# Six first-layer steps made ahead and held, first k by two queues, masks shared with GpSimd, the activation-table request moved, new order

## The chip, the cores and the metric

The kernel runs on one core of one Trainium2 chip. The metric is the device time of one execution in microseconds (us). TensorE is PE in the profile, VectorE DVE, ScalarE ACT, GpSimd POOL, and SyncE's queue of transfers SP.

## The reference

Attention with a window and a few global keys, then a gated two-layer network on the result:

```python
scores = scale * np.matmul(q, k.transpose(0, 1, 3, 2))       # 4 batches, 8 heads, 768 rows, 64 wide
bias = -slopes[:, None, None] * dist[None, :, :]             # dist: |row - column|, or n_local for global keys
scores = np.where(keep, scores + bias, -1000000000.0)
a = np.exp(scores - np.max(scores, axis=-1, keepdims=True))
a = a / (np.sum(a, axis=-1, keepdims=True) + 1e-09)
x = np.matmul(a, v)                                          # as 3072 tokens of 512
h = x @ w_in                                                 # 512 -> 2048
sp = np.where(h > 20.0, h, np.log1p(np.exp(np.minimum(h, 20.0))))
out = (h * np.tanh(sp)) @ w_out                              # 2048 -> 512
```

## The kernel before, in words

The 3072 tokens are cut into 12 chunks of 256 rows (three to a batch). For a chunk there are 8 attention pieces of two heads and 128 rows each: `scores` (PE), `largest` (DVE: adds the mask, takes the row's extreme), `exps` (ACT: `Exp` with the row sum), a turn of the matrix, and `weigh` (PE, with v). The first three chunks do this in f32 and turn on PE; later ones split every factor into a high and a low f16 half (`high_a` on ACT or DVE, `low_a` on POOL or DVE) and turn by DMA.

The network takes a chunk in 8 steps, so there are 96 steps, numbered m. A step makes 256 hidden columns:

- `moe_in` (i): 24 matmuls into the PSUM tile `ph`, of which there are two.
- `exp_h` (j), `square_e` (u), `ln_u` (n), `inverse_u` (r): four ACT instructions of 128x512, with the functions Exp, Square, Ln and Exp, in this order for every step (lines 548, 552, 556, 560).
- `times_h` (G) and `times_r` (H) on DVE, the latter waiting for `inverse_u`.
- `high_g` (z) and `low_g` (Z): two f16 halves; then `moe_out` (o): 24 matmuls into the output's sums.

The weights come as 32 raw pieces of 64-bit words and are converted on the chip, by `exponent_w`, `sign_w`, `bits_w`, `join_w`, `high_w` and `low_w` on ACT, DVE and POOL (A, S, B, C, D, E); that stands beside the attention of the first chunks (the last piece's halves are written at 144 us).

Which instruction stands where on each engine is written out by hand: a string `PROGRAM` of some two thousand tokens is read from left to right. A token is a letter (the function) with a number (the step or piece), and a stroke after it picks the second engine (DVE in place of ACT for copies, DVE in place of POOL for low halves). The order of the tokens is the order on each engine. `J`, `e` and some other letters below are tokens of this kind.

The built program loads a table set for ACT's functions with an instruction of its own, ACT_TABLE_LOAD. Line 141 asks for one set, named for both Ln and Exp, ahead of everything. Where no such request covers a function, the toolchain puts a load in by itself. In the kernel before, the built program has one row ACT_TABLE_LOAD on ACT, that of line 141.

Of the kernel before, what the change touches and what calls it, by code (L numbers as in the profile page):

```python
# [11 lines left out]
F16 = mybir.dt.float16  # L12
# [8 lines left out]
P = 128  # L21
# [93 lines left out]
def windowed(st, tc, loc):  # L115
# [16 lines left out]
    WB = 4  # L132

# [7 lines left out]
    nc.scalar.preload_act_table_set("natural_log_exp_and_others")  # L141
# [21 lines left out]
    def load_qk(G):  # L163
        if G >= 2 * NC:
            return
        ci, g = divmod(G, 2)
        b, c = divmod(ci, NCHB)
        o = OWN if c == 0 else 0
        pairs = slice(g * GH // 2, (g + 1) * GH // 2)
        qr = raws.tile([P, GH // 2, CH], F32, name="qr", bufs=4)  # L170
        kr = raws.tile([P, GH // 2, KW], F32, name="kr", bufs=4)
        nc.sync.dma_start(qr, L.qT[b].rearrange("(a j) d s -> (j d) a s", j=2)[:, pairs, c * CH:(c + 1) * CH])
        for j in range(2):
            half = slice(j * D, (j + 1) * D)
            nc.sync.dma_start(kr[half, :, o:], L.kd[ci, half].rearrange("p (a j) w -> p a j w", j=2)[:, pairs, j, o:])
        raw[G] = (qr, kr)
# [73 lines left out]
    jj = mt.tile([P, P], F32, name="u")  # L250
# [5 lines left out]
    d0 = mt.tile([P, P], F32, name="r")  # L256
    k0 = mt.tile([P, P], F32, name="r")
# [5 lines left out]

    def masks_own():
        nc.vector.tensor_scalar(off, rel, 0.0, None, op0=ALU.is_lt)
        nc.vector.scalar_tensor_tensor(off, rel, L.nlf, off, op0=ALU.is_ge, op1=ALU.max)
# [4 lines left out]
        nc.vector.scalar_tensor_tensor(d0, k0, FAR, d0, op0=ALU.mult, op1=ALU.max)  # L271

    def masks_far():

# [6 lines left out]

    def mask_own(h, other=False):
        copy(mb0[:, h, :], d0, -L.slopes[h] * UNIT, other)

    def mask_far(h, other=False):
        copy(mb[:, h, :], rel, -L.slopes[h] * UNIT, other)
# [258 lines left out]

    def exp_h(m):
# [76 lines left out]
    def checks(i):  # L623
# [32 lines left out]
        "i": moe_in, "j": exp_h, "u": square_e, "n": ln_u, "r": inverse_u, "G": times_h, "H": times_r,  # L656
# [217 lines left out]
```

## Time and profile before

| what | value |
| --- | --- |
| median of 3 runs | 626.84 us (624.49 to 627.2) |
| the profiled execution's own time | 625.97 us |
| its span, first to last instruction | 624.2 us |
| PE, DVE, ACT, POOL busy | 97%, 72%, 72%, 25% of the span |
| ACT_TABLE_LOAD | 1, of 1283 ns, at 0.82 us |
| ACT's four functions of a step | 96 times each |

The profile counts an engine as busy while an instruction of its runs; waits and the issue of transfers are not counted. A wait is put down to what ended it. Matmuls are pipelined and their ends modelled, so a busy PE is not a PE at its peak. Line numbers are those of the kernel before.

### The profile page before, as it was taken

To read this page: it belongs to the slowest core of one execution; us is meant where nothing else is said; L and a number is where in the kernel's file an instruction comes from. 1 tells how busy PE (TensorE), PEld (TensorE's weight loads), DVE (VectorE), ACT (ScalarE), POOL (GpSimd) and SP (SyncE) were. 2 spreads that over 40 slices of the span, in tenths; PEclk is the share of its full clock that TensorE was granted. 3 is DMA by queue.
4 is the path that set the end of the run, shared out by engine and by line. 5 is a ranking of instruction groups with operands and counts; after the bars stand their busy time and mean duration, and the time that the engine had idled before them with its cause. 6 is when DMAs were issued, how large, how long until landed. Compare 5 with 4: busy or idle time off the path is not lost.

```text
span 624.2 us, 13611 instructions
## 1 busy us (share of the span) xinstructions
PE 605.9 (97%) x5066; PEld 418.3 (67%) x5066; DVE 448.8 (72%) x1192; ACT 451.3 (72%) x1109; POOL 154.2 (25%) x130
## 2 busy tenths in 40 slices
PE   5999999989999999999999999999999999999996
PEld 3887766646766675667666677666667667667672
DVE  6999998995798677884659796657785685542443
ACT  4999988696777777877776774669757877545652
POOL 0021343341301322423141122112123344111020
PEclk9999999999999999999999999999999999999999
DMA  8997763422595574748088668045342256300001
GB/s 216 323 264 248 220 192 102 125 64 54 100 209 130 119 157 85 117 82 196 1 191 153 112 136 174 35 96 128 60 67 84 55 95 132 81 1 1 34 1 37
DMA packets 123014, 73.02 MB, mean 117 GB/s; under 512 B 91712, under 2 KB 112192, under 8 KB 122944
## 3 DMA queue, kind: packets, MB, share of 16 engines
q1 hardware_dynamic: 122944, 72.11, 49.6%
q8 instruction: 41, 0.67, 0.5%
q14 instruction: 29, 0.24, 0.1%
HBM read 39.85 MB, written 6.29 MB: 74 GB/s over the span
## 4 chain that ended last, share of the span: by engine, by line
PE 79%; DVE 11%; DMA 5%; ACT 3%; issue 2%; DVEq 0%; ACTq 0%
PE po L586 34%; PE ph L541 34%; PE sc L399 5%; PE pav L478 4%; DMA wts<-w_out 3%; DVE ws L349 2%; DMA qr<-qT 2%; DVE ws L345 1%; DVE wts L154 1%; DVE gf L564 1%; PE pav L586 1%; DVE A L413 1%; PE po L452 1%; DVE gf L568 1%; DVE ws L339 1%
## 5 line engine op out<-in xcount | busy, mean ns | idle before, releaser
L541 PE MATMUL ph<-xT,wts 128*128 128x256 f16 x2304 | 264.5, 273 | 0.9 <-DVE gf L564 0.8
L541 PEld LDWEIGHTS <-wts 128*128 128x128 f16 x2304 | 222.9, 98 | 36.6 <-issue 2.8
L586 PE MATMUL po<-wts,gt 128*128 128x512 f16 x1056 | 241.2, 381 | 3.2 <-DVE wts L154 1.3
L586 PEld LDWEIGHTS <-gt 128*128 128x128 f16 x1152 | 110.4, 98 | 128.8 <-issue 8.2
L154 POOL TENSOR_TENSOR gt<-gf,gt 128x512 f16<-128x512 f32 x59 | 71.6, 1215 | 226.4 <-ACT gt L150 99.1
L548 ACT ACTIVATE e<-ph 128x512 f32<-128x512 f32 x96 | 56.7, 590 | 87.0 <-PE ph L541 86.0
L568 DVE CUSTOM_DVE_ANT_0 gf<-gf,r 128x512 f32<-128x512 f32 x96 | 77.8, 811 | 56.6 <-ACT r L560 53.5
L422 ACT ACTIVATE A<-A,nm 128x256 f32<-128x256 f32 (+1 forms) x192 | 91.4, 478 | 21.8 <-DVE nm L413 19.4
L564 DVE SCALAR_TENSOR_TENSOR gf<-e,ph 128x512 f32<-128x512 f32 x96 | 65.3, 681 | 35.3 <-ACT e L548 35.2
L413 DVE CUSTOM_DVE_ANT_0 A<-sc,mb 128x256 f32<-128x256 f32 (+1 forms) x192 | 68.0, 396 | 24.5 <-PE sc L399 22.7
L154 POOL TENSOR_TENSOR hl<-A,hl 128x512 f16<-128x512 f32 (+1 forms) x37 | 44.1, 1197 | 147.7 <-DVE hl L148 93.6
L560 ACT ACTIVATE r<-r 128x512 f32<-128x512 f32 x96 | 60.0, 625 | 2.1
L552 ACT ACTIVATE u<-e 128x512 f32<-128x512 f32 x96 | 59.9, 626 | 2.0
L556 ACT ACTIVATE r<-u 128x512 f32<-128x512 f32 x96 | 59.7, 624 | 1.9
L154 POOL TENSOR_TENSOR wts<-ws,wts 128x512 f16<-128x512 f32 x17 | 21.3, 1260 | 75.8 <-ACT wts L150 56.1
L422 ACT ACTIVATION_READ_ACCUMULATOR A<-A,nm 128x1 f32 x192 | 36.1, 188 | 0.0
L150 ACT ACTIVATE gt<-gf 128x512 f16<-128x512 f32 x41 | 25.3, 620 | 13.5 <-DVE gmax L568 12.3
L478 PEld LDWEIGHTS <-AT 128*128 128x128 f16 x792 | 28.7, 98 | 6.9 <-issue 2.1
L154 DVE TENSOR_TENSOR gt<-gf,gt 128x512 f16<-128x512 f32 x37 | 27.3, 739 | 3.8 <-ACT gt L150 3.6
L489 DVE CUSTOM_DVE_ANT_1 x<-pav,ri 128x512 f32<-128x512 f32 x24 | 16.6, 691 | 17.4 <-PE pav L478 15.0
L148 DVE TENSOR_SCALAR hl<-A 128x512 f16<-128x512 f32 (+1 forms) x37 | 15.6, 424 | 17.8 <-ACT A L422 13.2
L399 PE MATMUL sc<-wc,ws 64*128 64x256 f16 (+1 forms) x432 | 28.1, 262 | 0.1
(114 smaller groups left out, 606.2 us busy)
## 6 DMA issues: line engine op xcount, KB each, us to landing
kr<-kd SPq DMA_DIRECT2D x32, 208.0 KB, 4.8
qr<-qT SPq DMA_DIRECT2D x24, 256.0 KB, 4.0
wts<-w_in SPq DMA_DIRECT2D x12, 512.0 KB, 8.4
wts<-w_out SPq DMA_DIRECT2D x12, 512.0 KB, 8.8
out<-ob SPq DMA_DIRECT2D x11, 512.0 KB, 3.2
vr<-v SPq DMA_DIRECT2D x9, 512.0 KB, 4.2
vc<-vo SPq DMA_DIRECT2D x15, 192.0 KB, 3.3
kr<-kd SPq DMA_DIRECT2D x16, 144.0 KB, 4.1
```

Of the source, the lines that this page charges most:

```text
L154: (nc.vector if other else nc.gpsimd).tensor_tensor(out, in_, high, op=ALU.subtract)
L399: nc.tensor.matmul(sc[j][:, a2, 0:w], x[half, a2, rows_], y[half, a2, col0:col0 + w], start=(n == 0), stop=(n == len(terms) - 1))
L413: nc.vector.tensor_tensor_reduce(out=A[:, j, 0:w], in0=sc[j][:, 0:w], in1=m, scale=-1.0 / (UNIT if ci < CF32 else UNIT * SQ), scalar=3.0e3 ...
L422: nc.scalar.activation(A[:, j], A[:, j], AF.Exp, bias=nm[:, h:h + 1], scale=-1.0, accum_out=rs[:, h:h + 1])
L541: nc.tensor.matmul(ph[:, j, :].rearrange("p (b t) -> p b t", b=2), wv4[:, 2 * fb, x, c * P:(c + 1) * P], xT[:, :, y * NCC + c, :], start=( ...
L548: nc.scalar.activation(mish[m]["e"], mish[m]["h"], AF.Exp, scale=-1.0 / (SV * SW), accum_out=esum[:, m:m + 1])
L552: nc.scalar.activation(u, mish[m]["e"], AF.Square, bias=0.5)
L556: nc.scalar.activation(mish[m]["r"], mish[m]["u"], AF.Ln, bias=0.25 / RS, scale=1.0 / RS)
L560: nc.scalar.activation(r, r, AF.Exp, scale=-1.0)
L564: nc.vector.scalar_tensor_tensor(gf, mish[m]["e"], 0.5, mish[m]["h"], op0=ALU.add, op1=ALU.mult)
L568: nc.vector.tensor_tensor_reduce(out=gf, in0=gf, in1=mish[m]["r"], scale=SG / (SV * SW * RS), scalar=0.0, op0=ALU.mult, op1=ALU.max, accum ...
L586: nc.tensor.matmul(pos[ci][t], gt[:, x, j, t * P:(t + 1) * P], wv4[:, 2 * fb + 1, y, :], start=(fb == 0 and n == 0), stop=(fb == NFB - 1 a ...
```

## The change

- The request for the table set is no longer made ahead of everything: it has become a token, `e`, and stands once, as `e0`, behind the last token of the program.
- Layer 1 of steps 16 to 21 (the third chunk's first six) is made early, among the steps of the first two chunks. Its result is copied out of PSUM by the new function `hold_h` (J) into SBUF, two of the copies into the output's buffer `ob`, four into tiles `hs`; `exp_h` and `times_h` of those steps then read it there. Two of the copies to `ob` and two to `hs` are ACT's, two to `hs` DVE's.
- The second half of the first k comes by ACT's queue instead of SP's.
- The masks' outside test is made in two parts, the own block's first, and with the stroke the masks of heads 4 to 7 are made by POOL in place of DVE.
- `ln_u` and `inverse_u` work in place in `u` (three buffers) instead of a tile `r` (two); q and k have three raw buffers instead of four.
- The order of `PROGRAM` is new up to about step 83, with other choices of engine; from there on the tokens are the same.

```diff
+    HELD = range(2 * NFP, 2 * NFP + 6)
...
-    nc.scalar.preload_act_table_set("natural_log_exp_and_others")
...
-        qr = raws.tile([P, GH // 2, CH], F32, name="qr", bufs=4)
-        kr = raws.tile([P, GH // 2, KW], F32, name="kr", bufs=4)
+        qr = raws.tile([P, GH // 2, CH], F32, name="qr", bufs=3)
+        kr = raws.tile([P, GH // 2, KW], F32, name="kr", bufs=3)
...
-            nc.sync.dma_start(kr[half, :, o:], L.kd[ci, half].rearrange("p (a j) w -> p a j w", j=2)[:, pairs, j, o:])
+            (nc.scalar if G == 0 and j else nc.sync).dma_start(kr[half, :, o:], L.kd[ci, half].rearrange("p (a j) w -> p a j w", j=2)[:, pairs, j, o:])
...
+    def outside(cols):
+        nc.vector.tensor_scalar(off[:, cols], rel[:, cols], 0.0, None, op0=ALU.is_lt)
+        nc.vector.scalar_tensor_tensor(off[:, cols], rel[:, cols], L.nlf, off[:, cols], op0=ALU.is_ge, op1=ALU.max)
...
+    def masked(out, in_, h, other):
+        if other and h >= H // 2:
+            nc.gpsimd.tensor_scalar(out, in_, -L.slopes[h] * UNIT, None, op0=ALU.mult)
+        else:
+            copy(out, in_, -L.slopes[h] * UNIT, other)
...
+    def hold_h(m, other=False):
+        k = m - HELD[0]
+        if k < 2:
+            if k == 0:
+                obs["h"] = mt.tile([P, 2, DM], F32, name="ob", bufs=1)
+            hs = obs["h"][:, k].rearrange("p (j t) -> p j t", j=2)
+        else:
+            hs = mt.tile([P, 2, CH], F32, name="hs", bufs=len(HELD) - 2)
+        copy(hs, mish[m]["h"], 1.0, other)
+        mish[m]["h"] = hs
...
-        u = mish[m]["u"] = mt.tile([P, 2, CH], F32, name="u")
+        u = mish[m]["u"] = mt.tile([P, 2, CH], F32, name="u", bufs=3)
...
-        mish[m]["r"] = mt.tile([P, 2, CH], F32, name="r")
+        mish[m]["r"] = mish[m]["u"]
...
+        "e": lambda i: nc.scalar.preload_act_table_set("natural_log_exp_and_others"),
...
-        u95 G95 n95 z94 r95 o93 Z94 H95 z95 o94 k1 Z95' o95 k2 Q11
+        u95 G95 n95 z94 r95 o93 Z94 H95 z95 o94 k1 Z95' o95 k2 Q11 e0
```

Where ACT's instructions stand in the built programs. First the start of ACT in the kernel before: L141 is the request for the set, L150 a helper's copy (`mb` are masks), L422 `exps`.

```order
L141 ACT_TABLE_LOAD
L150 ACTIVATE mb_99<-r 128x128 x2
L150 ACTIVATE mb<-e 128x256 x2
L150 ACTIVATE mb_99<-r 128x128
L422 ACTIVATE A,rs_163<-A,nm_164 128x128 x4
```

The same place in the changed kernel, where `exps` is line 430:

```order
L175 DMA kr<-kd 64x2x288
L150 ACT_TABLE_LOAD
L150 ACTIVATE mb_98<-u 128x128 x3
L150 ACTIVATE mb<-e 128x256
L150 ACTIVATE mb_98<-u 128x128
L430 ACTIVATE A,rs_147<-A,nm_148 128x128 x2
```

The load has moved behind ACT's own transfer, and it now belongs to line 150, a copy: it is one that the toolchain put there.

The second place is the last two steps on ACT, where the tokens of the two programs are the same. Before, L548, L552, L556 and L560 are Exp, Square, Ln and Exp of a step (the numbers behind the names tell the buffers apart), and `gt` is a copy of `high_g`:

```order
L548 ACTIVATE e_8361,esum_105<-ph_8308 128x512
L552 ACTIVATE u_8363<-e_8361 128x512
L556 ACTIVATE r_8367<-u_8363 128x512
L560 ACTIVATE r_8367<-r_8367 128x512
L548 ACTIVATE e_8383,esum_105<-ph_8336 128x512
L552 ACTIVATE u_8385<-e_8383 128x512
L556 ACTIVATE r_8389<-u_8385 128x512
L150 ACTIVATE gt_8391<-gf_8365 128x512
L560 ACTIVATE r_8389<-r_8389 128x512
```

In the changed kernel the four are lines 567, 571, 575 and 579:

```order
L567 ACTIVATE e_8279,esum_104<-ph_8226 128x512
L571 ACTIVATE u_8281<-e_8279 128x512
L575 ACT_TABLE_LOAD
L575 ACTIVATE u_8281<-u_8281 128x512
L579 ACT_TABLE_LOAD
L579 ACTIVATE u_8281<-u_8281 128x512
L567 ACTIVATE e_8300,esum_104<-ph_8254 128x512
L571 ACTIVATE u_8302<-e_8300 128x512
L575 ACT_TABLE_LOAD
L575 ACTIVATE u_8302<-u_8302 128x512
L150 ACTIVATE gt_8307<-gf_8283 128x512
L579 ACT_TABLE_LOAD
```

A table load now stands ahead of the Ln of a step and another ahead of the Exp that follows. In the whole list of ACT there are 186 such rows where there was one: 92 at the Ln (L575), 74 at the Exp behind it (L579), 9 at the Exp of the next step (L567), 9 at `exps` (L430), the first (L150) and the last (L672), which is the token `e0`.

The third place is ACT among the weights of the first chunks, where one of the six results is held. The rows are of the changed kernel; there is no row `ob<-ph` before. `wts`, `ws` and `wc` are weights on their way through the conversion, `vo` is v.

```order
L150 ACTIVATE vo<-vr 128x2x512
L349 ACTIVATE ws<-wr 128x512
L349 ACTIVATE ws<-wts 128x512
L150 ACTIVATE wts<-ws 128x512
L150 ACTIVATE ob<-ph 128x512
L349 ACTIVATE ws<-wts 128x512
```

The copy empties one of the two `ph` tiles; the step's own Exp (`e,esum<-ob`) stands 75 rows further on in this list.

More of the change, by code (lines that the diff above doesn't have):

```diff
@@ L255, in windowed @@
     off = mt.tile([P, W], F32, name="e")
-    d0 = mt.tile([P, P], F32, name="r")
-    k0 = mt.tile([P, P], F32, name="r")
+    d0 = mt.tile([P, P], F32, name="u", bufs=3)
+    k0 = mt.tile([P, P], F32, name="u", bufs=3)
     idn = cp.tile([P, P], F32, name="idn")
@@ L273, in masks_far @@
     def masks_far():
+        outside(slice(0, NPREV))
         nc.vector.tensor_scalar(off[:, NPREV:P], jj[:, 0:NGMAX], L.ngf, None, op0=ALU.is_ge)
@@ L280, in windowed @@
     mb0 = cp.tile([P, H, P], BF16, name="mb0")
+    def masked(out, in_, h, other):
[3 more added lines that the diff above has]
+            copy(out, in_, -L.slopes[h] * UNIT, other)
     def mask_own(h, other=False):
-        copy(mb0[:, h, :], d0, -L.slopes[h] * UNIT, other)
+        masked(mb0[:, h, :], d0, h, other)
     def mask_far(h, other=False):
-        copy(mb[:, h, :], rel, -L.slopes[h] * UNIT, other)
+        masked(mb[:, h, :], rel, h, other)
     def units(i):
@@ L655, in windowed @@
         "A": exponent_w, "S": sign_w, "B": bits_w, "C": join_w, "D": high_w, "E": low_w,
-        "i": moe_in, "j": exp_h, "u": square_e, "n": ln_u, "r": inverse_u, "G": times_h, "H": times_r,
+        "i": moe_in, "J": hold_h, "j": exp_h, "u": square_e, "n": ln_u, "r": inverse_u, "G": times_h, "H": times_r,
         "z": high_g, "Z": low_g, "o": moe_out, "Q": evacuate, "Y": store, "f": lambda i: flags(), "k": checks,
@@ L700, in windowed @@
-        j62 t72 u62 U17 z61 t73 V17 n62 Z61' r62 s74 G62 j63 v11 o60 a23' y72 c21' y73 t74 g72' g73 H62 u63 p72 o61 z62 X72 n63 Z62' y74 t75 x10 y75 g74'
-        p73' p74 s76 i64 r63 t76 t77 X73 y77 G63 y76 H63 X74 W72 d21' g76 o62 j64 p76 u64 g75' X76 z63 p75 n64 g77' r64 i65 X75 b23 G64 H64 Z63' W73 s78
-        p77' X77 o63 t78 a24 j65 z64' b24 u65 t79 n65 G65 y78 i66 r65 H65 z65' g78' W76 j66 W75 p78 s80 Q7 W74 t81 Z64 i67 X78 u66 c22' y79 t80 g79 n66 p79'
-        s82 r66 Z65' X79 W77 j67 o64 y80 y81 g80' G66 g81' o65 H66 R18 z66 u67 Z66 p81' n67 i68 r67 T18' p80' U18 X80 W78 X81 W79 R19 o66 G67 T19 j68 H67
@@ new lines, in windowed @@
+        B18 Z2' U5 C20 o10 i11 o2 i16 D16 A17 D20 j11 u11 n11 r11 h3 z3' E16' C18 S24' D15' Z3' E15 A24' E20' B24 B17 C24 G11 S25 S17 D18 E18 H11 J16 C17
+        B25 D24' l3 A25' E24 w19 w26 w23 v4 w30 q8 w21 o3 i12 i4 S22 A19 z11 c7 j12 C25 B19 G12 u12 n12 j4 A22 S19 B22 N0 C22 D17' Z11 E17 D22 u4 n4 a7 r12
+        r4 D25 G4 d7 b7 E22' C19 o11 i18 i17 s24 E25 H4 t24 A26' t25 J18 S26 z4 J17 D19 B21 B26 H12 z12' i5 s26 i13 t26 Z12' E19' B23 Z4 y25 g25 j5 j13 G5
+        B28 A23' u13 A21 S21 u5 n5 r5 S28 y24 C26 A28' p25' S23' C21 D26' C23 E26' S30' B30 G13 A30' y26 g24 g26' D21' E21 p24' H5 o12 o4 i20 i6 w29 X24 w27
@@ new lines, in windowed @@
+        w31 J20 D23 n13 j6 z5' Z5' C30 C28 t27 D30 D28 u6 n6 r6 r13 E23 i19 A29' J19' G6 B27 h4' S29' B29 H13 o5 i14 i21 A27 A31 z13 j14 S27' C27 E28 p26
+        Z13' G14 H6 E30' u14 a8 z6 n14 Z6' c8' J21' B31 D27' E27' i7 i15 r14 S31 c9 j7 u7 n7 r7 j15 a9 H14 b8 C31 z14' G7 C29 d8' Z14' H7 u15 D29 D31 j16
+        y27 n15 r15 X26 q10 x3 X25 q9 o13 o6 o14 s28 E31' G15 z7' E29 Z7 H15 z15' j17 u16 n16 r16 u17 Z15 G16 t28 t29 H16 o7 o15 n17 y28 r17 j18 d9 G17 z16'
+        Q0 u18 j19 b9 g28' Z16' p28' Y0 H17 n18 X28 G18 u19 s30 z17' r18 o16 Z17 c10 H18 l4 z18 a10 j21 Z18' v5 o17 Q1 q11 y29 g29 g27' p27' G19 G21 n19 t30
@@ new lines, in windowed @@
+        W24 o18 r19 p29' y30 t31 X29 H19 u21 z19 W25 W26 n21 X27 Z19' s32 r21 g30' W28 y31 p30 i22 j20 g31' X30 t33 p31 u20 H21 G20 o19 X31 j22 z21' u22
+        d10' Z21 n22 t32 n20 W29 r20 i23 y32 H20 z20' y33 R6 Z20 s34 T6' j23 U6 a11 W27 t35 o20 V6 u23 r22 G22 H22 G23 z22 W31 n23 Z22 W30 R7 o21 T7 g33 U7
+        y35 p33 V7 o22 r23 g35' g32 b10 X33 p35 t34 p32 X35 s36 i24 t36 X32 y36 H23 c11' Y1 z23' x4 t37 Z23 i25 j24 b11 g36 y37 o23 j25 u25 G25 G24 n25 u24
+        h5' r25 p36' i27 y34 H25 X36 n24 r24 Q2 W33 H24 W32 s38 z24' z25 Z24' i26 g37' g34 p37' p34 X37 Z25 t39 o24 j26 t38 j27 d11 q12 l5 u27 y38 o25 u26
@@ new lines, in windowed @@
+        n26 G27 r26 c12' y39 G26 W35 H26 i28 g39 X34 n27 z26' a12' Z26 g38' q14 W37 j28 p38 W36 x5 r27 s40 u28 p39 H27 o26 n28 t40 z27 r28 Z27' X38 R8 o27
+        X39 G28 T8 y40 U8 t41 y41 W34 i29 g41' H28 p41 b12 z28 Z28 s42 j29 W38 u29 t43 i30 g40 d12' n29 p40 r29 G29 a13 H29 X40 W39 c13' j30 o28 R9 z29 V8
+        u30 Z29 t42 T9 G30 y43 v6 d13 U9 i31 n30 r30 g43' V9 p43' H30 s44 X41 j31 z30' o29 u31 t45 X43 n31 G31 r31 y45 q15 H31 i32 z31' t44 Z30' Y2 b13 q13
+        o30 j32 y42 g42 g45' p45' G32 h6' X45 u32 p42' i34 n32 a15' l6 y44 r32 g44' x6 s46 j34 W43 t47 W40 y47 i33 H32 X42 t46 u34 y46 Z31' z32' c14' n34
@@ new lines, in windowed @@
+        Z32 o31 p44' j33 u33 Q3 g47' p47' W41 G34 s48 X44 G33 n33 W45 o32 r33 r34 H33 z33' g46' Z33 t49 i36 H34 t48 d14 z34 p46' y49 Z34' X46 o33 j36 y48
+        G36 X47 g49' u36 p49 n36 o34 r36 a14 H36 g48' s50 i35 i37 j35 z36 G35 u35 b14 Z36 n35 t51 r35 i38 p48 y51 H35 z35' j37 t50 Z35 u37 G37 y50 W44 g51'
+        W46 R10 s52 n37 W47 j38 W42 T10' o35 X49 r37 U10 H37 V10 p51' z37 t52 c15 Z37 o36 a16' v7 u38 X51 n38 R11 r38 X48 G38 o37 T11' U11 H38 V11 b15 d15'
+        i39 t53 y53 z38' g50' b16 p50 s54 j39 i40 u39 G39 Z38 X50 y52 n39 q16 r39 H39 W49 o38 z39' Y3 t55 Z39 y55 c16 o39 j40 d16 g53 G40 g52 u40 p52' n40
@@ new lines, in windowed @@
+        p53 i41 t54 X52 r40 y54 H40 z40' Q4 g54' Z40 W51 s56 j41 X53 u41 i42 g55' o40 j42 G41 a17 p55' u42 G42 n41 r41 W52 i44 n42 H41 h7 z41' t56 Z41 r42
+        t57 W48 p54' j44 W53 i45 H42 u44 X54 y57 G44 R12 n44 z42 s58 j45 Z42 o41 t59 u45 T12 g57' G45 r44 y56 U12 H44 W50 n45 i43 g56' X55 z44' r45 p56 H45
+        q17 l7 p57 o42 j43 Z44' V12 u43 y59 G43 X57 g59 a18' i46 n43 p59 r43 z45 X59 Z45' W54 c17' i47 X56 t58 H43 z43 j46 Z43 W55 u46 G46 s60 R13 n46 o43
+        y58 T13' t61 j47 y61 U13 b17 V13 o44 g58 G47 r46 p58 t60 q19 y60 H46 d17 g61' o45 z46 x7 u47 b18 n47 Z46' r47 i49 H47 g60' z47 p60 p61 X60 W57 j49
@@ new lines, in windowed @@
+        z62 h10' Z62 U17 t76 i63 V17 y76 l10 X75 b24 o62 j63 u63 n63 g74 g76' p76 d21 G63 y77 i65 p74' g77 r63 p77 H63 X77 i64 j65 q22 z63 u65 Z63' X74 s78
+        j64 o63 u64 G64 X76 G65 n64 n65 t78 r65 y78 H65 W77 i66 r64 H64 t79 y79 z64' W75 g78' W74 Z64 Q7 s80 W76 p78 t81 i67 j66 y81 R18 u66 T18' c22 z65'
+        o64 Z65' n66 j67 G66 t80 u67 n67 U18 o65 b22 r67 V18 r66 G67 g79' X78 p79' H66 i68 X79 z66' g81' Z66 H67 v11 d22' p81 W78 j68 o66 u68 n68 X81 z67 Y7
+        s82 x10 W79 t82 a23 i69 y82 Z67' r68 g82' G68 y80 t83 o67 H68 R19 z68 j69 Z68 T19' u69 s84 n69 G69 o68 r69 U19 g80 b23 V19 y83 p82' p80' X82 i70 t85
@@ new lines, in windowed @@
+        y85 t84 X80 H69 c24 g85' z69' i71 j70 Z69 u70 G70 h11' n70 r70 o69 H70 j71 z70' g83' Z70 p85 s86 o70 p83 X83 t86 y86 d24' W81 u71 W82 G71 X85 i74
+        n71 c23' y84 d23 r71 i73 j74 u74 G74 H71 n74 t87 r74 i72 g84' j73 z71' p84 u73 n73 Z71 X84 r73 g86 s88 j72 p86 o71 t88 u72 H74 y87 G73 g87 t89 y88
+        p87 W84 H73 W80 W83 z74' n72 W85 X87 r72 Z74' i75 G72 X86 g88' H72 p88' s90 j75 X88 i76 u75 t91 t90 R20 W87 z73' z72 y89 Z72 Q8 o72 T20 Z73 y91 n75
+        y90 o73 g89 j76 p89 u76 G76 G75 o74 n76 r75 r76 g91 H76 g90 l11 x11 s92 p90 W86 U20 i77 p91 X89 H75 R21 X90 i78 j77 t93 z75 Y8 u77 Z75' X91 z76' Z76
@@ new lines, in windowed @@
+        o75 j78 V20 T21 y93 n77 g93' o76 G77 p93 r77 u78 H77 z77' t92 W88 G78 i79 Z77' U21 V21 o77 j79 X93 n78 G79 u79 n79 r78 s94 y92 H78 i80 z78' r79 Z78
+        g92 H79 z79' Z79' o78 t95 t94 y94 g94 W89 W91 j80 o79 u80 y95 n80 g95' G80 p95 r80 W90 i81 Q9 H80 p94 p92' z80 X94 Z80 i83 j81 X92 u81 G81 X95 o80
+        j83 Y9 u83 n81 r81 W92 H81 W93 R22 i82 z81' Z81 W94 j82 W95 T22 o81 G82 n83 U22 r83 G83 V22 u82 n82 i84 r82 H82 R23 z82 i85 j84 T23' Z82' u84 U23
+        n84 H83 V23 r84 z83' o82 G84 j85 u85 H84 n85 Z83' G85 r85 o83 z84' H85 Z84 i86 o84 j86 z85 G86 u86 Z85' n86 r86 i87 H86 z86 Z86 o85 j87 u87 G87 n87
@@ L716, in windowed @@
+        r87 i88 H87 z87 Z87 i89 o86 j89 j88 u88 G88 n88 o87 r88 u89 H88 n89 z88' Z88' r89 Q10 G89 i90 H89 Y10 z89' Z89 o88 j90 u90 G90 n90 r90 i91 H90 o89
+        j91 u91 G91 n91 r91 i92 H91 z91' z90' Z91 Z90 i93 j92 G92 o90 j93 u92 n92 r92 u93 o91 H92 n93 G93 r93 k0 z92' Z92' H93 i94 z93' Z93 i95 j94 u94 G94
+        n94 r94 o92 H94 j95 u95 G95 n95 z94 r95 o93 Z94 H95 z95 o94 k1 Z95' o95 k2 Q11 e0
     """
```

73 lines of the change are left out of this document (19 added, 54 removed).

## Prediction

> **What bounds the kernel now.** First the page: its span, the busy time of the engines, and the chain of work that ended last.
>
> ```profile
> span 624.2 us, 13611 instructions
> PE 605.9 (97%) x5066; PEld 418.3 (67%) x5066; DVE 448.8 (72%) x1192; ACT 451.3 (72%) x1109; POOL 154.2 (25%) x130
> PE 79%; DVE 11%; DMA 5%; ACT 3%; issue 2%; DVEq 0%; ACTq 0%
> ```
>
> PE is busy nearly throughout and carries the chain; ACT has 624.2 - 451.3 = 172.9 us to spare. Whether that is so everywhere shows in five stretches (the first number is the length, then each engine's busy time and instructions), and, below them, how many Ln instructions of `ln_u` fall into each, one for a step:
>
> ```profile
> 0.00:150.00 150.00, 138.37 (x1025) 102.39 (x1026) 135.05 (x365) 123.43 (x302) 40.98 (x39) 0.99 0.64 186
> 150.00:300.00 150.00, 149.23 (x1351) 102.34 (x1350) 109.36 (x292) 113.90 (x289) 38.48 (x32) 1.00 0.61 127
> 300.00:450.00 150.00, 150.00 (x1351) 101.55 (x1349) 110.04 (x295) 107.29 (x274) 34.69 (x27) 1.00 0.54 111
> 450.00:560.00 110.00, 110.00 (x959) 74.48 (x958) 72.07 (x185) 76.74 (x186) 32.01 (x25) 1.00 0.39 75
> 560.00:624.20 64.20, 58.27 (x388) 37.57 (x386) 22.24 (x56) 29.93 (x61) 8.08 (x7) 0.98 0.05 18
> ```
>
> ```profile
> 0.00:150.00 150.00, 9.84 (x16) 0.99 0.64 186
> 150.00:300.00 150.00, 16.11 (x26) 1.00 0.61 127
> 300.00:450.00 150.00, 15.55 (x25) 1.00 0.54 111
> 450.00:560.00 110.00, 11.92 (x19) 1.00 0.39 75
> 560.00:624.20 64.20, 6.30 (x10) 0.98 0.05 18
> ```
>
> ACT (the fourth busy time) has 26.6, 36.1, 42.7, 33.3 and 34.3 us free in the five. It can take that much more work in each, and no more, before it takes the bound from PE.
>
> **The moved table request.** The built program of the changed kernel has 186 rows ACT_TABLE_LOAD on ACT where there was 1: a load ahead of the Ln of 92 of the steps, a load back ahead of the next Exp, one at the start and one behind everything. Groups of ACT's instructions (busy us, mean ns):
>
> ```profile
> L141 ACT ACT_TABLE_LOAD x1 | 1.3, 1283 | 0.8 <-PEq L867 0.8
> L560 ACT ACTIVATE r<-r 128x512 f32<-128x512 f32 x96 | 60.0, 625 | 2.1
> L556 ACT ACTIVATE r<-u 128x512 f32<-128x512 f32 x96 | 59.7, 624 | 1.9
> L150 ACT ACTIVATE hl<-A 128x512 f16<-128x512 f32 x30 | 18.5, 619 | 1.4 <-DMA AT<-hl 1.1
> L150 ACT ACTIVATE vo<-vr 128x1024 f16<-128x1024 f32 x6 | 6.3, 1046 | 0.3 <-PE pav L478 0.3
> L150 ACT ACTIVATE hl<-A 128x256 f16<-128x256 f32 x5 | 2.0, 407 | 0.1
> ```
>
> The one load of the trace took 1283 ns. The first load after the change hides in ACT's wait for the first masks as it did before, and the last stands behind the end of the work; 184 remain, 236.1 us. ACT has 172.9 us free in all, so they can't hide. A step has 184/96 = 1.917 loads, 2.459 us. Stretch by stretch ACT then needs 123.4 + 16 x 2.459 = 162.8, 113.9 + 26 x 2.459 = 177.8, 107.3 + 25 x 2.459 = 168.8, 76.7 + 19 x 2.459 = 123.5, and 29.9 + 10 x 2.459 = 54.5 us. Only the last is under the stretch's length (64.2, set by PE and the end of the work). The four others are longer by 12.8, 27.8, 18.8 and 13.5, together 72.9: 624.2 + 72.9 = 697.1 us, if ACT never waits. The bound moves from PE to ACT for the first 560 us.
>
> Does a load cost more than its own 1283 ns? ACT's instructions overlap a little where they don't depend on each other (start, duration):
>
> ```profile
> 320.90 0.63 ACT L556 ACTIVATE r<-u 128x512 f32<-128x512 f32 x1
> 321.57 0.63 ACT L560 ACTIVATE r<-r 128x512 f32<-128x512 f32 x1
> 322.10 0.61 ACT L150 ACTIVATE hl<-A 128x512 f16<-128x512 f32 x1
> ```
>
> The Exp follows its Ln after 0.67 us, so between these two, where the load goes, there is no overlap to lose; the independent copy starts 0.53 us after a 0.63 us instruction, so there a load can break 0.10. Between 0 and 184 x 0.10 = 18.4 us; I take the middle, 9, since both kinds of place occur. Below nothing it can't be: a load does no work for the others.
>
> The Trainium skill, page "ScalarE: Activation LUTs", section "What ACT_TABLE_LOAD costs", gives the same 1283 ns, with which this trace agrees, and adds a drain of about 1380 ns for every switch, 2.66 us in all. No run here shows that drain; by it the sum below would be longer by about 184 x 1.38 - 10 = 244 us (an estimate).
>
> **ACT's other work.** Counted in the two orders, ACT has 14 instructions of 128x512 fewer (halves of the attention and weights go to DVE; the four held results that ACT copies are in this count): -14 x 0.62 = -8.7. Three `vo` fewer: -3 x 1.05 = -3.1. Six small copies and one mask more: between 0.41 and 0.62 each, +3.2. Together -8.6 us. All of it counts, since ACT is now the bound. What DVE takes over has cover: 172 us of DVE's span are free, if few of them in the first 150.
>
> **ACT's waits.** A bound engine still waits where the order ties it to another. What ended ACT's waits (us in total, times, longest), and DVE's longest:
>
> ```profile
> ACT e L548 <- PE ph L541: 86.0, 50, 5.5
> ACT A L422 <- DVE nm L413: 19.4, 14, 3.6
> ACT gt L150 <- DVE gmax L568: 12.3, 14, 1.5
> ACT xhl L150 <- DVE xmax L489: 9.2, 6, 3.4
> ACT wts L150 <- DVE ws L349: 5.4, 5, 2.4
> ACT mb L150 <- DVE r L271: 5.1, 1, 5.1
> ```
>
> ```profile
> DVE gf L568 <- ACT r L560: 53.5, 35, 3.7
> ```
>
> Half of the waiting, 86.0 us, was for PE's layer 1; with PE ahead this goes. The 5.1 us for the first masks stay. The next four, 46.3 together, are for DVE: between 0 and 46.3. I take 19.4, the row of `exps` alone: there DVE's `largest` can stand behind a `times_r` that itself waits for ACT's second Exp (DVE's 53.5 us above), and such loops stay when ACT is late, while the others lie behind work that finishes early once ACT lags.
>
> **The intended parts.** What they can save on PE:
>
> ```profile
> PE sc L399 <- DMA kr<-kd: 5.9, 2, 5.2
> PE po L586 <- DVE wts L154: 1.3, 1, 1.3
> PE po L586 <- DVE wts L148: 1.2, 1, 1.2
> ```
>
> ```profile
> 134.00:136.00 2.00, 0.78 (x3) 1.00 0.53 204
> 136.00:138.00 2.00, 0.71 (x3) 0.88 0.00 0
> 138.00:140.00 2.00, 2.00 (x6) 0.50 0.00 0
> ```
>
> ```profile
> 137.28 3.39 PE L586 MATMUL po<-wts,gt 128*128 128x512 f16 x8 [1.30 <-DVE wts L154]
> ```
>
> ```profile
> 194.22 2.59 PE po L586 x12
> ```
>
> Six steps made ahead take matmuls out of the time in which DVE is late with a weight: the two waits of 1.3 and 1.2 and what follows them. The three stretches of 2 us show PE's busy time, its count and the granted clock, which fell to 0.50 behind the waits; there 8 matmuls (start, duration) took 3.39 us where 12 take 2.59 later in the chain: 3.39 - 8/12 x 2.59 = 1.66. In all up to 4.2 us. The first k by two queues can save the second of PE's two waits for k, 5.9 - 5.2 = 0.7, at most; the first mask's wait above is late next. Both are gains of PE's and worth nothing while ACT is the bound: with 697 us on ACT, PE's 605.9 have 91 us of cover. The new copies of held results are in ACT's count. The masks on POOL lie beside an engine that is 25% busy. One raw buffer less for q and k, and `r` in `u`, could delay a load or an Exp; PE's and DVE's lag behind ACT covers that, and if the cover were gone it would show as ACT waiting for DVE, inside the 46.3.
>
> **The sum.** 697.1 - 8.6 + 5.1 + 19.4 + 9 = 722.0 us of span. The profiled execution took 625.97 for a span of 624.2, 1.8 more (the median of the runs is 626.84): 723.8, say **724 us**. This case's own range is 697.1 - 8.6 + 5.1 + 1.8 = 695 to 695 + 46.3 + 18.4 = 760.
>
> **The rivals.** *Loads in the stream are cheap.* The one that was measured is the first of the program; a later one might be short. Below (150 - 113.9)/(26 x 1.917) = 0.72 us a load every stretch keeps PE as its bound, and what is left are the intended savings: 626.0 - 4.2 - 0.7 = 621, faster than before. For it speaks that one cold row is all there is, against it that this row already had nothing to wait for and no other work beside it on ACT. Chance 5%. The same 621 would come if the chip ran one load only, because the set with both functions stays loaded; against that stands the built order, with its 186 rows. 2%. The Trainium skill, same page, section "Table sets: the hidden batching unit", says that Ln and Exp share `natural_log_exp_and_others`, so that Ln then Exp needs one load; by that rule this rival would be right, but it holds only for a program that asks for that set.
>
> *A load holds ACT for twice its time*, because ACT stands still for as long again. Then 184 x 1.283 = 236 us more, less the 10 that the last stretch has free: 724 + 236 - 10 = 950. Nothing in the trace speaks for it: behind its one load ACT had nothing to do until 7.2 us. The drain of the Trainium skill's page would lead here. 7%.
>
> *PE's clock.* An ACT-bound PE waits about 1 us in every step ((697 - 606)/96), and the rows of the intended parts show that it lost 1.66 us after two waits within 4 us. If that came in all 96 steps, PE would need 624.2 + 159 = 783, with 1.8 about 785 us; it decides from (722 - 624)/1.66 = 59 steps on. Against it: the drop came where PE was busy 0.78 and 0.71 of 2 us, while one wait of 1 us in 7 leaves it busy for 86%. 6%.
>
> **How the numbers follow.** The forecast has 80%, and its own range holds nearly all of that; to have 8 in 10 inside, the range takes in PE's clock as well: 695 to 790. Left out are 950 (7%), 621 (7%) and little else. About 0.5% (3 us) is what the runs' own spread (624.5 to 627.2) lets one tell from no change. Faster by more than that: 6%, the cheap loads; within: 1%; slower: 93%.
>
> **What would show it.** Right: some 184 ACT_TABLE_LOAD of about 1.28 us, ACT over 90% busy in every stretch to 560 us or so, the chain that ended last mostly on ACT, PE's waits on DVE's and POOL's `gf` and `gt` (which wait for ACT) 80 to 110 us in all, and the wait of ACT for `ph` nearly gone. The step on loads is wrong if their mean is under 0.7 or if ACT's idle time behind each is as long as the load; the step on waits if ACT idles more than 60 us; PE's clock, if the granted clock is below 0.9 in the stretches. The whole forecast fails if the trace has one load.

## The result and the profile after

The changed kernel takes 782.0 us (776.2 to 784.27), the kernel before 627.02: the ratio is 1.2445 with an interval of [1.2343, 1.2548]. It is slower by 24%. 782 lies in the range on record, 695 to 790, but 58 us above the forecast of 724 and above the 760 at which the sum's own range ends. All times below stand beside runs of the kernel before on the same chip, and the ratios are against those.

The page of the changed kernel, its span, the engines' busy time, and the granted clock of PE in 40 slices:

```profile
span 780.6 us, 13760 instructions
PE 654.6 (84%) x5066; PEld 429.9 (55%) x5066; DVE 454.6 (58%) x1200; ACT 682.4 (87%) x1284; POOL 169.6 (22%) x140
PEclk9999999998889898999989998999999998999998
```

ACT is now the busiest engine, with 682.4 us where it had 451.3, and PE has fallen from 97% to 84%. What ACT does with the added 231 us stands in its groups (busy us, mean ns, idle time before):

```profile
L575 ACT ACT_TABLE_LOAD x92 | 118.0, 1283 | 1.6
L579 ACT ACT_TABLE_LOAD x74 | 94.9, 1283 | 1.3
...
L567 ACT ACT_TABLE_LOAD x9 | 11.5, 1283 | 0.2
L430 ACT ACT_TABLE_LOAD x9 | 11.5, 1283 | 0.1
...
L150 ACT ACT_TABLE_LOAD x1 | 1.3, 1283 | 1.6 <-PEq L887 1.6
L672 ACT ACT_TABLE_LOAD x1 | 1.3, 1283 | 0.0
```

The 186 loads of the built order are there, each of exactly the 1283 ns of the single one before. How a load sits among its neighbours (start, duration):

```profile
402.45 0.63 ACT L575 ACTIVATE u<-u 128x512 f32<-128x512 f32 x1
403.10 1.28 ACT L579 ACT_TABLE_LOAD   x1
404.40 0.63 ACT L579 ACTIVATE u<-u 128x512 f32<-128x512 f32 x1
```

Ln at 402.45, the load 0.65 later, Exp 1.30 after the load's start. Nothing is added behind the load.

ACT is idle for 780.6 - 682.4 = 98.2 us. What ended its waits (us in total, times, longest):

```profile
ACT e L567 <- PE ph L549: 26.4, 16, 5.5
ACT A L430 <- DVE nm L421: 23.6, 17, 3.6
ACT gt L150 <- DVE gmax L587: 16.2, 16, 2.6
ACT ob L614 <- PE po L605: 4.6, 2, 3.7
ACT gt L150 <- DVE rs L493: 3.5, 1, 3.5
ACT mb L150 <- DVE u L273: 3.3, 1, 3.3
```

The wait for PE's layer 1 fell from 86.0 to 26.4; the waits for DVE's row maxima and for `times_r` (`gmax`) are as large as before or larger. DVE in its turn waits for ACT's second Exp for 192.4 us (53.5 before) and PE mostly at `moe_out`. In the page's row for `moe_out`, the second below, 63.4 us is PE's idle time ahead of it, and ACT's copy `gt` ended 15.6 of that, the largest part:

```profile
DVE gf L587 <- ACT u L579: 192.4, 71, 6.2
```

```profile
L605 PE MATMUL po<-wts,gt 128*128 128x512 f16 x1056 | 266.3, 404 | 63.4 <-ACT gt L150 15.6
```

The page's chain of waits reaches back only over 7% of the span here, so it is not used.

### The profile page after: what moved, and what is told of

It reads as the page before. It is cut to its first block, busy times and chain, and to the rows that moved or that the text cites. A ratio compares the mean times of both kernels' runs of the same rounds, so it can differ in the third digit from the quotient of the medians.

```text
span 780.6 us, 13760 instructions
## 1 busy us (share of the span) xinstructions
PE 654.6 (84%) x5066; PEld 429.9 (55%) x5066; DVE 454.6 (58%) x1200; ACT 682.4 (87%) x1284; POOL 169.6 (22%) x140
## 5 line engine op out<-in xcount | busy, mean ns | idle before, releaser
L605 PE MATMUL po<-wts,gt 128*128 128x512 f16 x1056 | 266.3, 404 | 63.4 <-ACT gt L150 15.6
L549 PE MATMUL ph<-xT,wts 128*128 128x256 f16 x2304 | 276.2, 279 | 21.6 <-DVE gf L583 11.6
L549 PEld LDWEIGHTS <-wts 128*128 128x128 f16 x2304 | 228.3, 100 | 65.3 <-issue 20.3
L587 DVE CUSTOM_DVE_ANT_0 gf<-gf,u 128x512 f32<-128x512 f32 x96 | 71.7, 747 | 192.8 <-ACT u L579 192.4
L154 POOL TENSOR_TENSOR gt<-gf,gt 128x512 f16<-128x512 f32 x55 | 67.5, 1229 | 356.1 <-DVE gt L148 218.9
L575 ACT ACT_TABLE_LOAD x92 | 118.0, 1283 | 1.6
L430 ACT ACTIVATE A<-A,nm 128x256 f32<-128x256 f32 (+1 forms) x192 | 91.6, 478 | 24.1 <-DVE nm L421 23.6
L579 ACT ACT_TABLE_LOAD x74 | 94.9, 1283 | 1.3
L583 DVE SCALAR_TENSOR_TENSOR gf<-e,ph 128x512 f32<-128x512 f32 x90 | 61.1, 682 | 46.3 <-ACT e L567 41.7
L421 DVE CUSTOM_DVE_ANT_0 A<-sc,mb 128x256 f32<-128x256 f32 (+1 forms) x192 | 68.0, 397 | 21.0 <-PE sc L407 11.1
L567 ACT ACTIVATE e<-ph 128x512 f32<-128x512 f32 x90 | 52.6, 585 | 26.6 <-PE ph L549 26.4
L575 ACT ACTIVATE u<-u 128x512 f32<-128x512 f32 x96 | 60.2, 630 | 1.1
L579 ACT ACTIVATE u<-u 128x512 f32<-128x512 f32 x96 | 59.5, 626 | 0.8
L154 POOL TENSOR_TENSOR wts<-ws,wts 128x512 f16<-128x512 f32 x22 | 29.2, 1333 | 114.9 <-DVE wts L148 41.2
L150 ACT ACTIVATE gt<-gf 128x512 f16<-128x512 f32 x40 | 24.9, 623 | 20.0 <-DVE gmax L587 16.2
L430 ACT ACTIVATION_READ_ACCUMULATOR A<-A,nm 128x1 f32 x192 | 36.0, 188 | 0.0
L407 PEld LDWEIGHTS <-ws 64*128 64x128 f16 x432 | 19.5, 96 | 29.9 <-issue 27.0
```

Of the source, the lines that this page charges most:

```text
L154: (nc.vector if other else nc.gpsimd).tensor_tensor(out, in_, high, op=ALU.subtract)
L407: nc.tensor.matmul(sc[j][:, a2, 0:w], x[half, a2, rows_], y[half, a2, col0:col0 + w], start=(n == 0), stop=(n == len(terms) - 1))
L421: nc.vector.tensor_tensor_reduce(out=A[:, j, 0:w], in0=sc[j][:, 0:w], in1=m, scale=-1.0 / (UNIT if ci < CF32 else UNIT * SQ), scalar=3.0e3 ...
L430: nc.scalar.activation(A[:, j], A[:, j], AF.Exp, bias=nm[:, h:h + 1], scale=-1.0, accum_out=rs[:, h:h + 1])
L549: nc.tensor.matmul(ph[:, j, :].rearrange("p (b t) -> p b t", b=2), wv4[:, 2 * fb, x, c * P:(c + 1) * P], xT[:, :, y * NCC + c, :], start=( ...
L567: nc.scalar.activation(mish[m]["e"], mish[m]["h"], AF.Exp, scale=-1.0 / (SV * SW), accum_out=esum[:, m:m + 1])
```

## The experiments

Twelve kernels. "Idle" is ACT's: the span less its busy time. Ratios are against the kernel before on the same chip, with their intervals.

| run | loads that ran | ACT busy | span | idle | granted clock | median us | ratio |
| --- | --- | --- | --- | --- | --- | --- | --- |
| before | 1 | 451.3 | 624.2 | 172.9 | 0.996 | 627.02 | |
| after | 186 | 682.4 | 780.6 | 98.2 | 0.941 | 782.0 | 1.2445 [1.2343, 1.2548] |
| e1 asked first | 1 | 443.9 | 621.2 | 177.3 | 0.999 | 623.69 | 0.9932 [0.9903, 0.9961] |
| e2 asked behind k | 1 | 443.9 | 624.8 | 180.9 | 0.998 | 625.01 | 0.9949 [0.9925, 0.9972] |
| e3 before, asked last | 190 | 693.7 | 769.7 | 76.0 | 0.944 | 778.1 | 1.2408 [1.2360, 1.2456] |
| e4 two ahead | 193 | 691.8 | 785.0 | 93.2 | 0.938 | 788.28 | 1.2556 [1.2508, 1.2603] |
| e5 one behind (two written) | 97 | 568.9 | 656.2 | 87.3 | 0.990 | 658.6 | 1.0490 [1.0434, 1.0546] |
| e6 one ahead | 97 | 566.0 | 673.3 | 107.3 | 0.987 | 676.99 | 1.0777 [1.0723, 1.0830] |
| e7 two ahead (three written) | 193 | 692.0 | 788.1 | 96.1 | 0.938 | 790.08 | 1.2560 [1.2498, 1.2621] |
| e8 filler | 186 | 683.4 | 795.6 | 112.2 | 0.979 | 799.54 | 1.2729 [1.2658, 1.2801] |
| e9 three apart | 289 | 818.5 | 911.4 | 92.9 | 0.888 | 909.44 | 1.4495 [1.4412, 1.4578] |
| e10 two off the chain | 193 | 700.6 | 771.3 | 70.7 | 0.950 | 773.44 | 1.2337 [1.2263, 1.2411] |
| e11 times late | 186 | 679.0 | 739.5 | 60.5 | 0.954 | 742.06 | 1.1829 [1.1758, 1.1900] |
| e12 zero filler | 186 | 682.3 | 774.4 | 92.1 | 0.971 | 776.56 | 1.2377 [1.2305, 1.2450] |

### Is it the table request alone?

e1 takes the changed kernel and puts the request back to its old line:

```diff
+    nc.scalar.preload_act_table_set("natural_log_exp_and_others")
     ones = cp.tile([P, 1], F32, name="ones")
...
-        u95 G95 n95 z94 r95 o93 Z94 H95 z95 o94 k1 Z95' o95 k2 Q11 e0
+        u95 G95 n95 z94 r95 o93 Z94 H95 z95 o94 k1 Z95' o95 k2 Q11
```

> The changed kernel with the request for the set back ahead of everything (one load). Theory L, the loads and the waits they bring are the whole loss: 621 us, from 615 to 626, the 4.2 + 0.7 us of the intended parts saved. Rival O, the new order and the held results add waits of their own, and the 58 us by which the time lay over the forecast are theirs: about 680 us.

Measured: 623.69 us, a ratio of 0.9932. Everything else in the change together is a gain of 0.7%, clear of the interval, and the rival O is out: with one load, the order and the held results cost no time. (They do add waits of ACT for DVE's row maxima, 30.2 us where it was 19.4, but ACT has slack there.) The two waits of PE for late weights (1.3 and 1.2 us before) are gone from its list:

```profile
PE sc L408 <- DMA kr<-kd: 6.4, 1, 6.4
PE po L606 <- POOL gt L155: 1.7, 2, 1.0
PE po L461 <- ACT A L431: 1.0, 1, 1.0
```

e2 puts the request second, behind ACT's transfer of the first k:

```diff
-        q0 x0 w2 v0 s0 I0
+        q0 e0 x0 w2 v0 s0 I0
```

> The same with the request as second token, behind ACT's transfer of the first k. Theory L: as with the request first, within 0.5%; if the 1.28 us of the load ahead of the transfer matter, up to 1.3 us faster. Rival O: about 680 us as well.

Measured: 625.01 us, 0.9949. Its interval overlaps that of e1; where the one load stands at the start makes no difference that these runs can tell.

e3 goes the other way: the kernel before, and only the request moved behind everything (token `e0` behind `Q11`, the line at the top removed).

> The kernel before with nothing changed but the request moved behind everything. Theory L: ACT's work becomes 451.3 + 189 x 1.283 = 693.8 us; with the same idle time as in the changed kernel (780.6 - 682.4 = 98) the time is about 792 us, from 775 to 810. Rival O: the old order lacks the added waits, so about the forecast's 724 + 9 = 733 us.

Measured: 778.1 us; ACT is busy for 693.7 us, as worked out. The interval of its ratio, [1.2360, 1.2456], overlaps that of the changed kernel. The moved request alone makes the old kernel as slow as the new one.

e4 has the request first and loads put in by hand, one ahead of the Ln and one ahead of the second Exp of every step:

```diff
...
+        nc.scalar.preload_act_table_set("natural_log_exp_and_others")
         nc.scalar.activation(mish[m]["r"], mish[m]["u"], AF.Ln, bias=0.25 / RS, scale=1.0 / RS)
...
+        nc.scalar.preload_act_table_set("natural_log_exp_and_others")
         nc.scalar.activation(r, r, AF.Exp, scale=-1.0)
```

> The changed kernel with the request first and, in every step, one load put ahead of the Ln and one ahead of the Exp behind it: 192 loads at fixed places in place of the toolchain's 184. Theory L: 782 + 8 x 1.283 = 792 us, from 782 to 805. Rival, the change of set is what costs and not the load (here the same set is loaded over and over): well under 782, down to 621.

Measured: 788.28 us, with loads of 1283 ns. In the built program of the changed kernel the loads take two sets in turn, one at the Ln and another ahead of the next Exp; in that of e4 all of them take the one set that is there. So a load of the set that is loaded already costs what a change of set costs. With that the cause of the 24% is shown in both directions: taking the loads out removes it, putting loads in makes it.

### What makes ACT idle for 98 us?

The forecast had some 43 us of idle time for ACT. The next runs ask for what the rest is.

e6 puts in one load a step only, ahead of the Ln:

> The request first and one load ahead of every Ln: 96 x 1.283 = 123 us more on ACT, which by the stretches of the kernel before fit (147 of 150 us in the second, 139 of 150 in the third). If only the sum of ACT's work counts: 624 to 630 us. If ACT's waits come already with an ACT that is nearly full: 640 to 670.

Measured: 676.99 us. The work alone would have fitted into every stretch, so the first expectation fails, and the second is passed as well. ACT does 566.0 us of work in 673.3 and idles for 107.3: already with one load a step ACT can't be filled.

e5 was to put two loads behind the second Exp, where the step's chain has ended:

```diff
...
         nc.scalar.activation(r, r, AF.Exp, scale=-1.0)
+        nc.scalar.preload_act_table_set("natural_log_exp_and_others")
+        nc.scalar.preload_act_table_set("natural_log_exp_and_others")
```

> The request first, and in every step two loads put behind the second Exp, none between Ln and Exp: ACT's work is that of the run with the two loads ahead. Theory A, ACT's 98 us of idle time are waits of the written order and ACT's work is the bound: 788 us as with the loads ahead, from 775 to 800. Rival B, the idle time comes from the longer chain of a step (the loads stand between the step's first Exp and the one that times_r waits for): the chain is 2.6 us shorter, and of 98 us of idle time about 40 remain, 730 us.

Measured: 658.6 us, and the trace has 96 loads there, not 192:

```profile
L581 ACT ACT_TABLE_LOAD x96 | 123.2, 1283 | 1.6
```

The built program has 97 loads too, the request and one a step: of two requests in direct succession the toolchain puts in only one, so neither theory was tested as written. As a run with one load a step it is the counterpart of e6: nearly the same work (568.9 us of ACT against 566.0), 18.4 us less time. The place of the load counts, not only its length.

e7 fell to the same: one of its three loads stood right behind another and is not in the built program.

> The request first and three loads in a step: 123 us more than the run with two. Theory A: ACT is the bound and its idle time stays, 788 + 123 = 911, from 900 to 915. Rival C, the idle time is PE's and DVE's lateness (PE's clock among it), which shrinks when ACT is slower still: 870 to 890.

Measured: 790.08 us with 193 loads run, which repeats e4 and says nothing on three.

e9 does it with the three ahead of Square, Ln and the second Exp:

```diff
...
+        nc.scalar.preload_act_table_set("natural_log_exp_and_others")
         nc.scalar.activation(u, mish[m]["e"], AF.Square, bias=0.5)
...
```

> The request first and three loads in every step, now each ahead of another function (Square, Ln, second Exp), so that none stands behind another: 96 x 1.283 = 123 us more on ACT than with two ahead (785.0 us of span, 691.8 busy, 93 idle). Theory A, about 93 us of ACT's idle time belong to the written order: 788 + 123 = 911, from 900 to 920. Rival C, the idle time is the others' lateness and shrinks as ACT slows: 870 to 890.

Measured: 909.44 us, theory A's number. Its page:

```profile
span 911.4 us, 13864 instructions
...
PE 695.4 (76%) x5066; PEld 443.5 (49%) x5066; DVE 451.8 (50%) x1200; ACT 818.5 (90%) x1387; POOL 168.3 (18%) x140
```

With one, two and three loads ahead of the functions of a step ACT idles 107.3, 93.2 and 92.9 us. From two loads on every microsecond of work on ACT is a microsecond of time, and the idle time on top hardly changes: it belongs to the order and to what its instructions wait for, not to an engine that is nearly fast enough.

e10 keeps two loads a step but takes both out of the step's chain: one behind the second Exp, one between the two Exp of an attention piece.

```diff
...
             nc.scalar.activation(A[:, j], A[:, j], AF.Exp, bias=nm[:, h:h + 1], scale=-1.0, accum_out=rs[:, h:h + 1])
+            if j == 0:
+                nc.scalar.preload_act_table_set("natural_log_exp_and_others")
...
         nc.scalar.activation(r, r, AF.Exp, scale=-1.0)
+        nc.scalar.preload_act_table_set("natural_log_exp_and_others")
...
```

> The request first and two loads to a step as in the run with two ahead, but one behind the step's second Exp and one between the two Exp of an attention piece: ACT's work is the same, the chain from a step's first Exp to its times_r is 2.6 us shorter. Theory A: 788 us, from 780 to 795. Rival B, the step's chain: one load a step cost 18.4 us less behind the second Exp than ahead of the Ln, so two loads 788 - 2 x 18.4 = 751 us.

Measured: 773.44 us, between the two. The idle time fell from 93.2 to 70.7 (ACT's busy time rose by 8.8, below). So the longer chain of a step is a part, some 22 us, and not the larger one. In the waits, those for DVE fell (nm 22.8 and gmax 13.3 in e4):

```profile
ACT e L570 <- PE ph L552: 22.2, 17, 3.2
ACT A L431 <- DVE nm L422: 9.3, 7, 3.5
ACT gt L151 <- DVE gmax L591: 5.1, 4, 2.6
```

e11 attacks the waits for DVE directly. `times_r` of a step takes the factor of the step made before, so that DVE needn't stand there until ACT's second Exp; this changes the computation in all steps but the first, and the work stays the same.

```diff
+    late_r = []
...
-        nc.vector.tensor_tensor_reduce(out=gf, in0=gf, in1=mish[m]["r"], scale=SG / (SV * SW * RS), scalar=0.0, op0=ALU.mult, op1=ALU.max, accum_out=gmax[:, m:m + 1])
+        late_r.append(mish[m]["r"])
+        nc.vector.tensor_tensor_reduce(out=gf, in0=gf, in1=late_r[-2] if m else late_r[0], scale=SG / (SV * SW * RS), scalar=0.0, op0=ALU.mult, op1=ALU.max, accum_out=gmax[:, m:m + 1])
```

> The changed kernel, but times_r of a step multiplies with the result of the step made before it (the output is not the reference's), so DVE does not stand waiting for ACT's second Exp. Theory E, ACT's idle time comes from DVE standing there with the row maxima and the next halves behind it: ACT's waits for DVE, 23.6 + 16.2 + 3.5 us, go, 739 us, from 715 to 750. Theory A in its plain form, the waits go over to others: 775 to 785.

Measured: 742.06 us, 40 less than the changed kernel and theory E's number. The waits of ACT in this run:

```profile
ACT e L567 <- PE ph L549: 19.2, 14, 2.8
ACT A L430 <- DVE nm L421: 7.0, 8, 2.1
ACT gt L150 <- DVE gmax L590: 6.3, 6, 2.6
```

Those for the maxima and for `times_r` went from 39.8 to 13.3, that for layer 1 from 26.4 to 19.2, and ACT's idle time from 98.2 to 60.5. DVE's wait for the second Exp, 192.4 us in the changed kernel, fell to 21.4. So some 38 us of ACT's idle time hang on that wait of DVE. How they hang on it is a loop: ACT hands a step's second Exp to DVE; DVE, which has stood waiting for it, has to do `times_r` and what is queued behind it before ACT gets its next row maximum or its next result of `times_r`. In the changed kernel's timeline one turn of it reads so (ACT's and DVE's rows):

```profile
360.36 1.28 ACT L579 ACT_TABLE_LOAD   x1
361.65 0.63 ACT L579 ACTIVATE u<-u 128x512 f32<-128x512 f32 x1
362.31 0.69 DVE L587 CUSTOM_DVE_ANT_0 gf<-gf,u 128x512 f32<-128x512 f32 x1 [4.56 <-ACT u L579]
...
363.05 0.43 DVE L148 TENSOR_SCALAR gt<-gf 128x512 f16<-128x512 f32 x1
363.39 0.42 DVE L421 CUSTOM_DVE_ANT_0 A<-sc,mb 128x256 f32<-128x256 f32 x1
...
363.85 0.51 ACT L430 ACTIVATE A<-A,nm 128x256 f32<-128x256 f32 x1 [1.57 <-DVE nm L421]
```

DVE stood 4.56 us for ACT's second Exp (L579), then did `times_r` (L587) and a copy `gt` ahead of the row maximum (L421), and ACT stood 1.57 us for that maximum. e11 also lets a step's result leave earlier, as e10 does, so its 38 us and the 22 of e10 are not two separate shares; what makes up the 60.5 us that remain was not tried.

### Is it PE's half clock?

The granted clock fell to 0.941, and the time, 782, is near the 785 that the prediction gave for this rival. e8 and e12 raise the clock with more work for PE. e8 puts ten matmuls ahead of every layer-1 step:

```diff
...
+        for _ in range(10):
+            nc.tensor.matmul(ph[:, 0, :].rearrange("p (b t) -> p b t", b=2), wv4[:, 4 * fp, 0, 0:P], xT[:, :, 0, :], start=True, stop=True)
...
```

> The changed kernel with 10 more matmuls of 128x256 ahead of those of every layer-1 step, written over by the first real one: 96 x 10 x 0.109 = 105 us more work for PE, which waited 118 us in the changed kernel, and a clock that should fall less often (granted 0.941 there). Theory D, PE's half clock makes layer 1 late and so ACT: a granted clock of 0.98 or more and 740 to 770 us. Theory A: the clock rises and the time stays at 782 or grows up to 800.

Measured: 799.54 us at a clock of 0.979. It speaks against theory D, but not cleanly: the filler makes layer 1 later, and ACT's wait for it rose from 26.4 to 44.0 us.

e12 puts the filler where PE stands anyway, ahead of `moe_out`, as products with zeros:

```diff
...
+        for n in range(3):
+            nc.tensor.matmul(pos[ci][0], zero, wv4[:, 2 * 2 * fp + 1, 0, :], start=(fp == 0 and n == 0), stop=False)
...
```

> The changed kernel with three more matmuls of 128x512 by a tile of zeros ahead of the real ones of every moe_out, where PE waited 63 us: 96 x 3 x 0.216 = 62 us more work for PE, but at the place where it stood, so that layer 1 is hardly later. Theory D, the half clock makes PE late and so ACT: the granted clock rises from 0.941 to 0.97 or more and the time falls to 740 to 770. Rival: the clock rises and the time stays within 1% of 782.

Measured: 776.56 us at a granted clock of 0.971:

```profile
core 0: 774.4 us, clock 0.971
```

Half of the lost clock is back, and the time is 0.7% shorter, which these runs can't tell from nothing (the intervals of the two ratios overlap; their far ends allow 2%). The 740 to 770 of theory D did not come. And e9 has the lowest clock of all, 0.888, with ACT's idle time no longer than with two loads a step. So PE's clock follows the waiting and is not the main cause of it; that the half which is still missing costs nothing was not tried.

## Why the prediction was right and where it was off

- **The loads don't hide, ACT takes the bound.** Right. 186 loads ran, 1283 ns each. ACT's work came to 682.4 us; the prediction's terms give 451.3 + 236.1 - 8.6 = 678.8. e1 and e3 show that the moved request makes the loss.
- **What a load costs beyond itself.** The 9 us were an upper end where the loads of the toolchain stand. ACT's busy time is 3.6 us over the prediction's terms, but these hold only 184 of the 185 added loads and price ACT's other work by a count of instructions. e1 measures that work: 443.9 us, one load among it. 443.9 + 185 x 1.283 = 681.3, and ACT was busy for 682.4, so only about 1 us was lost in overlaps. Where a function depends on the one before it, it starts 1.30 us after the load that stands between (e4 too). In e10, which moves both loads of a step, one of them between two Exp, ACT is busy for 8.8 us more than in e4: 0.09 us a step. So a broken overlap can cost about the 0.10 that the prediction read from the timeline, but in most places none is broken.
- **The rival with twice the time** (7%), and with it the drain that the Trainium skill names on the page "ScalarE: Activation LUTs", section "What ACT_TABLE_LOAD costs": out. The next function starts 1.30 us after the load, in the changed kernel as in e4. Here the trace differs from the page, and the measurement decides: 1283 ns and no drain, in a program whose loads take two sets in turn.
- **Cheap loads** (5%) and one load only (2%): out, by the same rows.
- **ACT's waits: the term that was mis-sized.** The sum had 9.7 us free in the last stretch and 5.1 + 19.4 + 9 of waits and overlaps, about 43 in all; ACT idled for 98.2. The row of `exps`, taken at 19.4, measured 23.6, and the loop that the prediction names there is real. The step that failed is the rest of that sentence, "I take 19.4, the row of `exps` alone ... while the others lie behind work that finishes early once ACT lags". They don't finish early: in this order DVE waits for ACT and ACT for DVE in turns, 16.2 us of ACT's waits are for `times_r`, and e11 shows that some 38 us of the 98 hang on DVE's wait for the second Exp. Nor did the wait for PE's layer 1 go; 26.4 of 86.0 us stayed, since PE stands at `moe_out` for halves that come late through DVE, with the next layer 1 behind. That second half was not tried by itself and stays argued. e9 shows that the idle time doesn't shrink when ACT gets slower still, so it had to be added in full to ACT's work, and the prediction's upper bound for the waits (46.3) was no bound, because it was read from a run in which ACT had slack. It was also read from the old order: with the loads in the old order (e3, profiled in the fastest of its runs) ACT idles for 76.0 us, in the new one for 98.2, so the new order seems to bring waits of its own once ACT is the bound. e3 is about as slow because it has more work for ACT, 693.7 us against 682.4.
- **PE's clock** (6%): the number, 785, was near, the mechanism wrong. The clock did fall to half in places (0.50 from 400 to 404 us), but with half of the loss given back (e12) the time stays within 0.7%. The range reached over 760 only for this rival. That 782 lies in it is therefore luck: the sum with its own bounds missed by 22 us.
- **The intended parts** were put at 4.2 + 0.7 us. e1 is 0.7% faster than the kernel before, about 4.3 us. The two waits for weights went. The first k by two queues did not bring the 0.7: the first eight scores run from 6.43 us in e1, where before two ran from 5.17 and the other six from 6.64; the transposes behind the first masks, which the prediction did not price, start at 8.65 instead of 9.69.
- **The signs to look for.** Right: the count and length of the loads, and a granted clock over 0.9 (0.92 to 0.97 in the stretches). The sign set against the step on waits, ACT idle for more than 60 us, came: 98.2. Wrong: ACT at over 90% in every stretch (it was 87% of the span); PE's waits for `gf` and `gt` of DVE and POOL, put at 80 to 110 us, were 48.7, and 64.3 with ACT's `gt`. Whether the chain that ended last is mostly ACT's can't be read from the 7% that it covers.
- **A slip.** DVE's free span was put at 172 us; it is 624.2 - 448.8 = 175.4. Nothing hangs on it.

## What to carry to other kernels

Look for ACT_TABLE_LOAD in the built order before any other number: a request for a table set that stands behind the functions it should cover is worth nothing, and the toolchain's own choice here switched twice a step. An engine that takes the bound over does so with the waits of an order that was made for another bound: count its idle time in a run in which it is nearly full (e6: 107 us with one load a step), not the list of its waits when it had slack. And of a change with several parts, run the parts apart: the 0.7% that the rest gains was hidden under 24%.

## What the runs showed of the hardware

- A table load takes 1283 ns whether it changes the set (the changed kernel, 186 loads) or loads the one that is there (e4, 192 loads).
- A function that follows a load starts 1.30 us after the load's start (the changed kernel and e4): nothing is added behind it.
- One load a step costs 18.4 us more ahead of the Ln than behind the second Exp (e6, e5), though ACT's work is 2.9 us less.
- A PE that is busy for 76% of the span was granted 0.888 of its clock (e9), one that is busy for 84% 0.941 (after), and one that is kept busy with products of zeros 0.971 (e12).
